# An attention and expert kernel on Trainium2: one weight piece per tile, the pieces' clamp on GpSimd, new charges in the planner, and the split of scores and value products four tiles earlier

## The chip, the cores and the metric

The kernel runs on one core of a Trainium2 chip. The metric is device time in microseconds of one execution. The engines are named as in the profile: PE is TensorE (its weight loads are PEld), DVE is VectorE, ACT is ScalarE, POOL is GpSimd, SP is SyncE, whose queue issues all DMAs here. The runs of the kernel before took 870.15 us in the median of three (869.43 to 871.0).

## What is computed

```python
k_all, v_all = concat(k_g, k_l), concat(v_g, v_l)          # 32 global and 512 local keys
out_g = softmax(q_g @ k_all.T / 8) @ v_all                 # 8 batches x 8 heads, head size 64
s_ll = where(abs(i - j) <= 32, q_l @ k_l.T / 8, -1e9)
out_l = softmax(concat(q_l @ k_g.T / 8, s_ll)) @ v_all
x = concat(out_g, out_l)  -> 8 x 544 tokens of 512
h = maximum(maximum(x @ w1, x @ w2), x @ w3)               # 512 -> 768
out = h @ w_out                                            # 768 -> 512
```

All activations are float32. The four expert weights come in as float64, 24 pieces of 128x512 in all (18 of w1 to w3, 6 of w_out), and are turned into pairs of rounded values on the chip.

## The kernel before

**Tiles.** Two heads make a pair, and a pair's 512 local queries make four tiles of 128. So there are 128 tiles, sixteen to a batch. For each tile the kernel computes scores of both heads against a window of at most 224 keys (`scores`), reduces them on DVE with the mask, the sign and the minimum (line 314), takes the exponential on ACT (316), scales on whatever engine the planner picks, mostly POOL (112), and sends the result by DMA into a padded tile `early` or `prob` (322). PE transposes that (334), the copy `pt` leaves PSUM (`trans`), the global queries' part is transposed and joined (`transg`, 355), and `pv` multiplies by the values (375 or 382). Once per pair `glob` and `glob_soft` do the global queries' scores, softmax and six DMAs into `probg`. At every fourth tile the pair's result is split for the experts (`split_x`, tile xs).

**Native and split products.** PE multiplies either plain float32 (`native`, lines 265, 307 and 375) or values split into a rounded high half and a rest (lines 269, 311 and 382). Splitting needs a copy and a subtraction for queries (qs), keys (kst), values (vs) and probabilities (pt), and for the value products three additions behind (388, 390). `NATK` holds the tiles whose scores are native, `NAT` the number of tiles whose value products are. Before, scores are native up to tile 27 and value products up to tile 25.

**Experts.** `moe_group` does a batch's three products and the maximum (413, 421), splits the result (h), and does the second product (432). It is a generator, of which `fill` runs 18 steps in each tile, one batch behind the attention: the first batch's experts start at tile 16. The weights of its block f are needed from about tile 16 + 2f, the second product's from tile 28.

**Weight pieces.** `convert` loads a piece (512 KB, tile wraw) and rebuilds float32 values from the float64 bits: the modulus on ACT (167), the clamp (168), the mask and shift (169) and two combinations (170, 171) on DVE. A step later it makes the high half (`copy`) and the rest (`sub`), wh and wl or woh and wol. `weight_step` finishes one piece, computes the next and loads another. `WS` says how many steps follow each tile. The load tiles share the buffers h0 to h5 with the experts: first six of them, later three, two and one.

**What sets the order.** The code issues work in the order of the tile loop, and a scheduler orders each engine's instructions from that. `copy`, `sub` and `times` choose their engine by charges kept in `load`: the engine with the least sum takes the work, and `spend` charges what is done without a choice. All engines work off their own queues in order. An instruction that waits holds up those behind it on its engine, and a DMA that waits on SP holds up the later ones.

Of the kernel before, what the change touches and what calls it, by code (L numbers as in the profile page):

```python
# [10 lines left out]
F32R = mybir.dt.float32r  # L11
# [3 lines left out]
ALU = mybir.AluOpType  # L15
# [4 lines left out]
DM, DF = 512, 768  # L20
# [2 lines left out]
KW = 576  # L23
NEG = -8.0e9

NATK = range(0, 28)
HIMAX = float(np.array(0x47EFFFFF, np.int32).view(np.float32))


# [18 lines left out]
def f32(ap):  # L48
    return ap.bitcast(F32)


def body(ctx, tc, kin, qin, vin, min_, w1, w2, w3, w4, out):
    nc = tc.nc
    act, dve, pool, pe = nc.scalar, nc.vector, nc.gpsimd, nc.tensor
# [21 lines left out]
    def spend(e, ns):  # L76
        load[e] += ns
# [18 lines left out]
    def copy(out, a, psum=False):  # L96
        n = width(out)
        c = {"d": n * (1.04 if psum else 0.52) + (160 if psum else 150), "a": n * 0.833 + (150 if psum else 190)}
        if least(c) == "d":
            dve.tensor_copy(out=out, in_=a)  # L100
        else:
            act.copy(out=out, in_=a)  # L102
# [32 lines left out]
    wo = []  # L135
# [3 lines left out]
    def pieces():  # L139
        n = 0  # L140
        for f in range(12):
            for i in range(3 if f < 6 else 1):
                if f < 6:
                    src = (w1, w2, w3)[i][:, f * 128:(f + 1) * 128].rearrange("(k p) f -> p k f", p=128)
                    yield src, 4, n, wh[f][:, i].rearrange("p k f -> p (k f)"), wl[f][:, i].rearrange("p k f -> p (k f)")
                else:
                    if f == 6:
                        wo.extend(const.tile([128, 6, DM], F32R, name=t, tag=t) for t in ("woh", "wol"))
                    yield w4[(f - 6) * 128:(f - 5) * 128], 1, n, wo[0][:, f - 6], wo[1][:, f - 6]
                n += 1  # L150

    def STAGE(n):
# [5 lines left out]
    def convert(piece):  # L158
        src, k, m, dh, dl = piece
        n, i = 512, STAGE(m)  # L160
        r = moe.tile([128, n], mybir.dt.int64, name="wraw", tag=f"h{i}")
        nc.sync.dma_start(out=r.rearrange("p (k f) -> p k f", k=k) if k > 1 else r, in_=src)
        hi = r.bitcast(I32).rearrange("p (n t) -> p n t", t=2)[:, :, 1]
        lo = r.bitcast(I32).rearrange("p (n t) -> p n t", t=2)[:, :, 0]
        yield
        c = cut[:, m % 6] if m < 18 else moe.tile([128, n], I32, name="wct", tag="o", bufs=2)
        act.activation(out=f32(c), in_=r.bitcast(F32).rearrange("p (n t) -> p n t", t=2)[:, :, 1], func=AF.Abs)
        dve.tensor_scalar(out=f32(c), in0=f32(c), scalar1=2.0 ** -15, scalar2=HIMAX, op0=ALU.max, op1=ALU.min)
        dve.tensor_scalar(out=c, in0=c, scalar1=0x07FFFFFF, scalar2=3, op0=ALU.bitwise_and, op1=ALU.logical_shift_left)
        dve.scalar_tensor_tensor(out=hi, in0=hi, scalar=-0x40000000, in1=c, op0=ALU.bitwise_and, op1=ALU.bitwise_or)  # L170
        dve.scalar_tensor_tensor(out=c, in0=lo, scalar=29, in1=hi, op0=ALU.logical_shift_right, op1=ALU.bitwise_or)
        spend("a", 520)
        spend("d", 1900)
        yield
        copy(dh, f32(c))
        sub(dl, f32(c), f32(dh))
        yield
# [20 lines left out]


    NS = 4 * B * NP  # L200
    NAT = 26
    EARLY, AHEAD = 16, 9
    kraw, kst, qraw, qs, vraw, vs, xr, sc, pg, pts = [{} for _ in range(10)]

# [49 lines left out]
    def glob(p, step):  # L254
        if p >= B * NP:
            return
        if step == 0:
            pg[p] = [att.tile([64, KW], F32, name="sg", bufs=1)[:, 0:NG], small.tile([64, 2], F32, name="nmg"), small.tile([64, 2], F32, name="zg")]
        s, nm, z = pg[p]
        c0, n = SEG[step]  # L260
        s0 = 384 * step
        ps = psS.tile([128, 512], F32, name="S")
        if 4 * p in NATK:

            pe.matmul(ps[0:64, 0:n], lhsT=kraw[p][:, KW:KW + 2 * SG], rhs=kraw[p][:, c0:c0 + n], start=True, stop=True)  # L265
            in1 = zero[0:64].to_broadcast([64, n])
        else:
            for j in range(2):
                pe.matmul(ps[:, 0:n], lhsT=qgz.rearrange("p j x -> p (j x)")[:, 128 * j:128 * j + 128],  # L269
                          rhs=kst[p][:, j, c0:c0 + n], start=(j == 0), stop=(j == 1))  # L270
            in1 = s[:, s0:s0 + n]
            copy(in1, ps[64:128, 0:n], True)
        dve.tensor_tensor_reduce(out=s[:, s0:s0 + n], in0=ps[0:64, 0:n], in1=in1, scale=-0.125, scalar=3.0e38,  # L273
                                 op0=ALU.add, op1=ALU.min, accum_out=nm[:, step:step + 1])
        spend("d", n * 1.04 + 75)

    def glob_soft(p):
        if p >= B * NP:
# [13 lines left out]
    def scores(sl):  # L292
        if sl >= NS:
            return
        p, t = divmod(sl, 4)
        c0, n = WIN[t]

        ps = pm.tile([128, 512], F32, name="pm") if sl < 12 else psS.tile([128, 512], F32, name="S")
        s = att.tile([128, 2, 224], F32, name="s", bufs=4)
        sc[sl] = early[:, sl % 6] if sl < EARLY else prob[sl % 2]  # L300
        nm = small.tile([128, 2], F32, name="nm")
        z = small.tile([128, 2], F32, name="z")
        ph = [ps[:, 0:224], ps[:, 224:448]]
        for j in range(2):
            if sl in NATK:

                pe.matmul(ph[j][:, 0:n], lhsT=qraw[sl][:, 128 * j:128 * j + 128], rhs=kraw[p][:, c0:c0 + n],  # L307
                          start=True, stop=True)
                continue
            for a in range(2):  # L310
                pe.matmul(ph[j][:, 0:n], lhsT=qs[sl][:, a, 128 * j:128 * j + 128],  # L311
                          rhs=kst[p][:, j, c0:c0 + n], start=(a == 0), stop=(a == 1))
        for j in range(2):
            dve.tensor_tensor_reduce(out=s[:, j, 0:n], in0=ph[j][:, 0:n], in1=mask[:, (1, 0, 1, 0)[t], 32 * (t == 0):32 * (t == 0) + n],  # L314
                                     scale=-0.125, scalar=3.0e38, op0=ALU.add, op1=ALU.min, accum_out=nm[:, j:j + 1])
            act.activation(out=s[:, j, 0:n], in_=s[:, j, 0:n], func=AF.Exp, bias=nm[:, j:j + 1], scale=-1.0,  # L316
                           accum_out=z[:, j:j + 1])
        dve.tensor_scalar(out=z, in0=z, scalar1=1e-9, scalar2=None, op0=ALU.add)
        dve.reciprocal(out=z, in_=z)
        for j in range(2):  # L320
            times(s[:, j, 0:n], s[:, j, 0:n], z[:, j:j + 1])
        nc.sync.dma_start(out=f32(sc[sl])[:, :, 0:n], in_=s[:, :, 0:n])
        spend("d", 2 * (n * 1.04 + 75) + 150)
        spend("a", 2 * (n * 0.833 + 278))

    def trans(sl):
# [130 lines left out]

    mm = [None]

    WS = [0, 0, 0, 1, 0, 1, 0, 1, 0, 1, 0, 1, 2, 2, 1, 2, 2, 1, 2, 2, 1, 2, 2, 1, 2, 2]  # L460

    def fill(n):
        if mm[0]:
# [34 lines left out]
    for sl in range(NS):  # L498
        p, t = divmod(sl, 4)
# [84 lines left out]
```

## Time and profile before

| what | value |
|---|---|
| runs | 870.15 us (869.43 to 871.0) |
| profiled execution, its own time | 868.76 us |
| its span, first to last instruction | 867.0 us |
| PE busy | 817.3 us (94%) |
| DVE, ACT, POOL busy | 617.3, 492.0, 502.9 us |
| mean granted clock of PE | 0.968 |

The span is that of the instructions; the execution's own time has 1.8 us around it. In the tables of busy time, a column is an engine's busy time in the stretch, and in brackets the number of its instructions; behind them stand the granted clock of PE as a share of full speed, the mean busy share of the 16 DMA engines, and GB/s. In the groups by shape, the row gives line, engine, operation, output and inputs, shape, count, then busy us and mean ns of one, then the idle time of the engine just before, with who ended it. A wait row gives the total, the number and the longest, in us.

### The profile page before, as it was taken

Reading aid. Unit: us, or ns where it says so; the run is one execution under the profiler, and the core shown is the slowest. Engines: PE = TensorE matmul, PEld = TensorE weight load, DVE = VectorE, ACT = ScalarE, POOL = GpSimd, SP = SyncE. Lnnn points to the kernel's source line nnn. Section 1 sums busy time; section 2 is a strip of 40 time slices with the busy share of each in tenths; the row PEclk is TensorE's granted clock in tenths of the full one; section 3 lists DMA queues with packets and bytes.
Section 4 is the critical chain, followed back from the end, with each engine's and each line's share of the span. In section 5 each row is a group of like instructions: output and inputs, shape, how many; then the busy total and the mean of one; then the engine's idle time right before and its main releaser. Section 6 shows DMA issues by size and latency. Waiting matters only on the chain.

```text
span 867.0 us, 15698 instructions
## 1 busy us (share of the span) xinstructions
PE 817.3 (94%) x4452; PEld 677.3 (78%) x4452; DVE 617.3 (71%) x1885; ACT 492.0 (57%) x1392; POOL 502.9 (58%) x669
## 2 busy tenths in 40 slices
PE   5865988799999999999999999999999999999997
PEld 3643766588888788888887888888888888888897
DVE  4678897887788787887788887877877877521111
ACT  3654655566666566766666666666666666411111
POOL 4544657576667666776767666756677665411211
PEclk8876889899999999999999999999999999999999
DMA  6676755334333533343333433353333422100000
GB/s 202 192 222 197 212 182 158 117 93 144 99 101 104 160 110 105 99 133 114 103 107 104 142 102 98 101 161 104 111 110 122 122 78 74 62 24 1 25 25 25
DMA packets 107238, 98.53 MB, mean 114 GB/s; under 512 B 21008, under 2 KB 97936, under 8 KB 107152
## 3 DMA queue, kind: packets, MB, share of 16 engines
q1 hardware_dynamic: 107152, 97.53, 37.0%
q8 instruction: 36, 0.59, 0.3%
q14 instruction: 50, 0.41, 0.2%
HBM read 56.85 MB, written 8.91 MB: 76 GB/s over the span
## 4 chain that ended last, share of the span: by engine, by line
PE 77%; DVE 10%; DMA 6%; issue 2%; POOL 2%; ACT 1%; SPq 1%; DVEq 0%; POOLq 0%; ACTq 0%
PE pm L413 45%; PE pm L432 13%; PE O L382 6%; PE S L311 5%; PE T L334 3%; DMA wraw<-w_in 1%; DMA wraw<-wo_in 1%; PE S L269 1%; DVE wraw L170 1%; DVE xs L100 1%; PE S L265 1%; PE S L355 1%; PE O L375 1%; DVE s L314 1%; DVE kst L94 1%
## 5 line engine op out<-in xcount | busy, mean ns | idle before, releaser
L413 PE MATMUL pm<-xs,wh 128*128 128x512 f32 (+1 forms) x1296 | 411.2, 390 | 0.0
L413 PEld LDWEIGHTS pm<-xs,wh 128*128 128x128 f32 x1296 | 235.3, 191 | 31.6
L413 PE MATMUL pm<-xs,wl 128*128 128x512 f32 (+1 forms) x648 | 254.9, 393 | 0.0
L112 POOL TENSOR_SCALAR s<-s,z 128x224 f32<-128x224 f32 (+1 forms) x243 | 111.6, 472 | 87.7 <-ACT lox L102 46.7
L316 ACT ACTIVATE s<-s,nm 128x192 f32<-128x192 f32 (+1 forms) x256 | 118.0, 462 | 48.6 <-DVE nm L314 44.0
L413 PEld LDWEIGHTS pm<-xs,wl 128*128 128x128 f32 x648 | 123.6, 191 | 23.5 <-issue 2.4
L432 PE MATMUL pm<-woh,h 128*128 128x512 f32 x408 | 135.2, 400 | 1.3 <-POOL h L94 1.1
L94 POOL TENSOR_TENSOR h<-m,h 128x512 fp32r<-128x512 f32 (+1 forms) x54 | 69.3, 1284 | 99.2 <-ACT h L102 99.2
L94 POOL TENSOR_TENSOR qs<-qraw,qs 128x256 fp32r<-128x256 f32 x100 | 79.5, 795 | 68.6 <-ACT qs L102 42.0
L421 DVE TENSOR_TENSOR m<-pm,m 128x512 f32<-128x512 f32 (+1 forms) x108 | 71.0, 657 | 63.0 <-PE pm L413 62.7
L94 DVE TENSOR_TENSOR pt<-T,pt 128x512 fp32r<-128x512 f32 x102 | 70.4, 691 | 36.2 <-ACT pt L102 33.8
L432 PEld LDWEIGHTS pm<-woh,h 128*128 128x128 f32 x408 | 74.6, 188 | 15.4 <-POOL h L94 4.3
L314 DVE CUSTOM_DVE_ANT_0 s<-S,mask 128x192 f32<-128x192 f32 (+1 forms) x232 | 77.5, 370 | 9.9 <-PE S L307 5.2
L432 PE MATMUL pm<-wol,h 128*128 128x512 f32 x204 | 81.7, 401 | 0.0
L94 POOL TENSOR_TENSOR vs<-vraw,vs 128x256 fp32r<-128x256 f32 x102 | 75.7, 743 | 9.0 <-ACT vs L102 4.2
L102 ACT CAST pt<-T 128x512 fp32r<-128x512 f32 x83 | 48.4, 583 | 47.6 <-PE T L334 47.6
L382 PEld LDWEIGHTS O<-pt,vs 128*128 128x128 f32 x408 | 66.4, 188 | 9.2
L382 PE MATMUL O<-pt,vs 128*128 128x320 f32 (+1 forms) x408 | 72.8, 299 | 0.0
L102 ACT CAST qs<-qraw 128x256 fp32r<-128x256 f32 x85 | 34.6, 407 | 64.3 <-PE S L311 64.0
L334 PEld LDWEIGHTS T<-identr,prob 128*128 128x128 f32 x448 | 51.3, 143 | 24.9 <-issue 5.0
L311 PEld LDWEIGHTS S<-kst,qs 128*128 128x128 f32 x400 | 59.5, 190 | 11.2 <-DVE nmg L273 2.8
L102 ACT CAST h<-m 128x512 fp32r<-128x512 f32 (+1 forms) x54 | 32.3, 597 | 60.5 <-DVE m L421 60.4
(99 smaller groups left out, 1340.5 us busy)
## 6 DMA issues: line engine op xcount, KB each, us to landing
vraw<-v_in SPq DMA_DIRECT2D x128, 128.0 KB, 2.6
qraw<-q_in SPq DMA_DIRECT2D x100, 128.0 KB, 2.2
prob<-s SPq DMA_DIRECT2D x56, 224.0 KB, 2.4
prob<-s SPq DMA_DIRECT2D x56, 192.0 KB, 2.3
wraw<-w_in SPq DMA_DIRECT2D x18, 512.0 KB, 4.5
out_dram<-o SPq DMA_DIRECT2D x32, 256.0 KB, 2.6
kraw<-k_in SPq DMA_DIRECT2D x25, 320.0 KB, 3.1
qn<-q_in SPq DMA_DIRECT2D x28, 128.0 KB, 3.5
```

Source lines behind the costliest of these rows:

```text
L94: (dve if least(c) == "d" else pool).tensor_tensor(out=out, in0=a, in1=b, op=ALU.subtract)
L100: dve.tensor_copy(out=out, in_=a)
L102: act.copy(out=out, in_=a)
L112: pool.tensor_scalar(out=out, in0=a, scalar1=col, scalar2=1.0, op0=ALU.mult, op1=ALU.mult)
L311: pe.matmul(ph[j][:, 0:n], lhsT=qs[sl][:, a, 128 * j:128 * j + 128], rhs=kst[p][:, j, c0:c0 + n], start=(a == 0), stop=(a == 1))
L314: dve.tensor_tensor_reduce(out=s[:, j, 0:n], in0=ph[j][:, 0:n], in1=mask[:, (1, 0, 1, 0)[t], 32 * (t == 0):32 * (t == 0) + n], scale=-0.12 ...
L316: act.activation(out=s[:, j, 0:n], in_=s[:, j, 0:n], func=AF.Exp, bias=nm[:, j:j + 1], scale=-1.0, accum_out=z[:, j:j + 1])
L334: i = pe.transpose(pr[:, 256 * j + 128 * c:256 * j + 128 * c + 128], s[:, j, 128 * c:128 * c + 128], identr)
L382: pe.matmul(o[:, j, 0:320].rearrange("p (a q) -> p a q", a=2)[:, :, 0:n], lhsT=vs[sl][:, 2 * j + c].rearrange("p a d -> p (a d)"), rhs=pt[ ...
L413: pe.matmul(ps[:, 0:n], lhsT=w[f][:, i, k], rhs=xs[k][:, a, 0:n], start=(q == 0), stop=(q == 11))
L421: dve.tensor_tensor(out=m[:, 0:n], in0=ps[:, 0:n], in1=m[:, 0:n], op=ALU.max)
L432: pe.matmul(ps, lhsT=hh[f][:, a, 128 * t:128 * t + 128], rhs=w[:, f], start=(q == 0), stop=(q == 17))
```

## The change

Five edits stand together.

1. `WS` gives one weight step behind each of the tiles 1 to 25, where it gave none up to tile 2, one behind every second tile up to 11, and then two, two and one in turn. Before, 24 pieces are through at tile 23, now at tile 25.
2. The clamp of a piece (before line 168) is issued on POOL, not on DVE. The instruction is the same, a maximum with one constant and a minimum with another.
3. The planner's charges change: a piece is charged 650 to ACT, 900 to POOL and 2100 to DVE (520 and 1900 before, nothing to POOL); a score reduction is charged 220 beyond its columns where it was 75, and the small reciprocal work 440 where it was 150. Since DVE's sum rises faster, `copy`, `sub` and `times` pick ACT and POOL more often, in the whole kernel.
4. `NAT` falls from 26 to 22 and `NATK` from 28 to 24 tiles: four tiles more have split value products and four more have split scores.
5. The tiles woh and wol are made when the first piece of w_out is finished, not when it is loaded.

```diff
--- before.py
+++ after.py
@@ -23,7 +23,7 @@
 KW = 576
 NEG = -8.0e9
 
-NATK = range(0, 28)
+NATK = range(0, 24)
 HIMAX = float(np.array(0x47EFFFFF, np.int32).view(np.float32))
 
 
@@ -144,9 +144,7 @@
                     src = (w1, w2, w3)[i][:, f * 128:(f + 1) * 128].rearrange("(k p) f -> p k f", p=128)
                     yield src, 4, n, wh[f][:, i].rearrange("p k f -> p (k f)"), wl[f][:, i].rearrange("p k f -> p (k f)")
                 else:
-                    if f == 6:
-                        wo.extend(const.tile([128, 6, DM], F32R, name=t, tag=t) for t in ("woh", "wol"))
-                    yield w4[(f - 6) * 128:(f - 5) * 128], 1, n, wo[0][:, f - 6], wo[1][:, f - 6]
+                    yield w4[(f - 6) * 128:(f - 5) * 128], 1, n, f - 6, None
                 n += 1
 
     def STAGE(n):
@@ -165,13 +163,18 @@
         yield
         c = cut[:, m % 6] if m < 18 else moe.tile([128, n], I32, name="wct", tag="o", bufs=2)
         act.activation(out=f32(c), in_=r.bitcast(F32).rearrange("p (n t) -> p n t", t=2)[:, :, 1], func=AF.Abs)
-        dve.tensor_scalar(out=f32(c), in0=f32(c), scalar1=2.0 ** -15, scalar2=HIMAX, op0=ALU.max, op1=ALU.min)
+        pool.tensor_scalar(out=f32(c), in0=f32(c), scalar1=2.0 ** -15, scalar2=HIMAX, op0=ALU.max, op1=ALU.min)
         dve.tensor_scalar(out=c, in0=c, scalar1=0x07FFFFFF, scalar2=3, op0=ALU.bitwise_and, op1=ALU.logical_shift_left)
         dve.scalar_tensor_tensor(out=hi, in0=hi, scalar=-0x40000000, in1=c, op0=ALU.bitwise_and, op1=ALU.bitwise_or)
         dve.scalar_tensor_tensor(out=c, in0=lo, scalar=29, in1=hi, op0=ALU.logical_shift_right, op1=ALU.bitwise_or)
-        spend("a", 520)
-        spend("d", 1900)
+        spend("a", 650)
+        spend("p", 900)
+        spend("d", 2100)
         yield
+        if m >= 18:
+            if not wo:
+                wo.extend(const.tile([128, 6, DM], F32R, name=t, tag=t) for t in ("woh", "wol"))
+            dh, dl = [w[:, dh] for w in wo]
         copy(dh, f32(c))
         sub(dl, f32(c), f32(dh))
         yield
@@ -198,7 +201,7 @@
 
 
     NS = 4 * B * NP
-    NAT = 26
+    NAT = 22
     EARLY, AHEAD = 16, 9
     kraw, kst, qraw, qs, vraw, vs, xr, sc, pg, pts = [{} for _ in range(10)]
 
@@ -272,7 +275,7 @@
             copy(in1, ps[64:128, 0:n], True)
         dve.tensor_tensor_reduce(out=s[:, s0:s0 + n], in0=ps[0:64, 0:n], in1=in1, scale=-0.125, scalar=3.0e38,
                                  op0=ALU.add, op1=ALU.min, accum_out=nm[:, step:step + 1])
-        spend("d", n * 1.04 + 75)
+        spend("d", n * 1.04 + 220)
 
     def glob_soft(p):
         if p >= B * NP:
@@ -320,7 +323,7 @@
         for j in range(2):
             times(s[:, j, 0:n], s[:, j, 0:n], z[:, j:j + 1])
         nc.sync.dma_start(out=f32(sc[sl])[:, :, 0:n], in_=s[:, :, 0:n])
-        spend("d", 2 * (n * 1.04 + 75) + 150)
+        spend("d", 2 * (n * 1.04 + 220) + 440)
         spend("a", 2 * (n * 0.833 + 278))
 
     def trans(sl):
@@ -457,7 +460,7 @@
 
     mm = [None]
 
-    WS = [0, 0, 0, 1, 0, 1, 0, 1, 0, 1, 0, 1, 2, 2, 1, 2, 2, 1, 2, 2, 1, 2, 2, 1, 2, 2]
+    WS = [0] + [1] * 25
 
     def fill(n):
         if mm[0]:
```

Line numbers behind line 147 move by up to 3: the clamp is line 166, mask and combinations are 167 to 169, the score reduction 317.

DVE's order just behind the sum over the columns of tile 7 (xg, line 392). `cut` and `wraw` are a piece in work, `wh` its high half, `s<-S,mask` a score reduction. Before:

```order
L392 TENSOR_REDUCE xg<-xr 128x32
L100 CAST wh_102<-cut 128x512
L168 TENSOR_SCALAR cut<-cut 128x512
L169 TENSOR_SCALAR cut<-cut 128x512
L170 SCALAR_TENSOR_TENSOR wraw<-wraw,cut 128x512
L171 SCALAR_TENSOR_TENSOR cut<-wraw 128x512
L100 CAST wh_103<-cut 128x512
L100 COPY pt<-S 128x2x32
L314 ISA s,nm<-S,mask 128x224
```

Now:

```order
L395 TENSOR_REDUCE xg<-xr 128x32
L167 TENSOR_SCALAR cut<-cut 128x512
L168 SCALAR_TENSOR_TENSOR wraw<-wraw,cut 128x512
L169 SCALAR_TENSOR_TENSOR cut<-wraw 128x512
L167 TENSOR_SCALAR cut<-cut 128x512
L168 SCALAR_TENSOR_TENSOR wraw<-wraw,cut 128x512
L169 SCALAR_TENSOR_TENSOR cut<-wraw 128x512
L317 ISA s,nm<-S,mask 128x224
```

Two pieces stand where one stood, without their clamps, and the casts and the copy of pt have gone from DVE.

POOL's order around the tiles 16 to 20, from the softmax of the global queries of the pair (sg) on. `wl`, `wol` are pieces' low halves, `kst`, `qs`, `qgz` are halves of keys and queries, `h` is of the experts. Before:

```order
L112 TENSOR_SCALAR sg<-sg,zg 64x544
L112 TENSOR_SCALAR s<-s,z 128x224 x2
L94 TENSOR_TENSOR wl_112<-cut,wh_106 128x512
L94 TENSOR_TENSOR qgz<-kraw,qgz 128x2x32
L94 TENSOR_TENSOR wl_113<-cut,wh_107 128x512 x2
L112 TENSOR_SCALAR s<-s,z 128x224 x2
L94 TENSOR_TENSOR h_1159<-m,h_1159 128x512
L94 TENSOR_TENSOR kst<-kraw,kst 64x576 x2
L94 TENSOR_TENSOR wl_113<-cut,wh_107 128x512
L112 TENSOR_SCALAR s<-s,z 128x192 x2
```

Now, from the first keys of the pair whose scores are split:

```order
L94 TENSOR_TENSOR kst<-kraw,kst 64x576 x2
L94 TENSOR_TENSOR wl_113<-cut,wh_107 128x512
L112 TENSOR_SCALAR s<-s,z 128x192 x2
L166 TENSOR_SCALAR cut<-cut 128x512 x2
L112 TENSOR_SCALAR sg<-sg,zg 64x544
L94 TENSOR_TENSOR h_1033<-m,h_1033 128x512
L94 TENSOR_TENSOR wl_113<-cut,wh_107 128x512
L94 TENSOR_TENSOR qs<-qraw,qs 128x256
L166 TENSOR_SCALAR wct<-wct 128x512
L112 TENSOR_SCALAR s<-s,z 128x224 x2
```

The clamps stand among the scalings and the low halves, one or two at a time, and the keys and queries of the split tiles come before the last pieces of w1 to w3 are finished.

## The prediction, on record before the result

> **What bounds the kernel now.** I read the page first (DVE, ACT and POOL are all partly idle, PE is not), then the table of busy time by stage, then the waits of PE in the stage in which the change lies, then the groups of instructions by shape. The stages are cut where the work changes. Up to 92.1 us stand the attention tiles 0 to 15, from there to 172.7 us the tiles 16 to 25, which run beside the first batch's expert layer, and behind 172.7 us everything is split attention beside expert matmuls, with a tail of experts alone.
>
> ```profile
> core 0: us, PE busy (x) PEld busy (x) DVE busy (x) ACT busy (x) POOL busy (x), PEclk, DMA share, GB/s
> 0.00:92.10 92.10, 60.23 (x326) 43.32 (x326) 62.88 (x221) 48.17 (x148) 45.12 (x67) 0.78 0.67 199
> 92.10:172.70 80.60, 70.32 (x363) 53.00 (x363) 68.30 (x162) 45.15 (x122) 52.22 (x53) 0.92 0.55 170
> 172.70:750.00 577.30, 574.49 (x3163) 483.73 (x3162) 464.43 (x1462) 379.62 (x1086) 388.51 (x533) 1.00 0.37 111
> 750.00:867.00 117.00, 112.27 (x605) 97.25 (x603) 21.66 (x43) 19.07 (x39) 17.07 (x18) 1.00 0.07 22
> ```
>
> I call these stages A (92.1 us), B (80.6 us), C and the tail. That A holds sixteen tiles and B ten is read from the native value products of line 375, eight records a tile (one straddles the cut):
>
> ```profile
> 0.00:92.10 92.10, 16.37 (x129) 10.36 (x129) 0.78 0.67 199
> 92.10:172.70 80.60, 7.37 (x80) 4.69 (x80) 0.92 0.55 170
> ```
>
> In C, PE is busy 574.49 of 577.30 us at full clock: there nothing but PE's own work counts. In A and B PE idles and its granted clock sinks to 0.78 and 0.92. So the change can pay only ahead of 172.7 us, or in what it takes off PE. What a tile costs when PE alone sets the pace is read where it is busy without a break, with the counts of line 375 and of the split value products of line 382 (four a tile) for the same stretches:
>
> ```profile
> 92.10:111.60 19.50, 19.50 (x110) 15.10 (x109) 16.88 (x44) 12.58 (x34) 11.82 (x12) 1.00 0.82 248
> 301.90:394.90 93.00, 92.76 (x513) 78.39 (x512) 74.72 (x238) 61.64 (x179) 64.30 (x88) 1.00 0.38 114
> ...
> 92.10:111.60 19.50, 2.18 (x24) 1.40 (x24) 1.00 0.82 248
> 301.90:394.90 93.00, 11.41 (x64) 10.41 (x64) 1.00 0.38 114
> ```
>
> Three native tiles take 19.50 us, 6.50 each. Sixteen split ones take 93.0, 5.81 each. Ten native tiles at 6.50 are 65.0 us, so B loses 15.6 of its 80.6 us to waits and to the low clock behind them. Who is waited for there, longest first:
>
> ```profile
> PE S L355 <- DVE nm L314: 3.0, 2, 2.1
> PE S L355 <- DMA probg<-sg: 2.8, 1, 2.8
> ```
>
> DVE is named, and it is busy 68.30 of 80.60 us in B, 0.85, the highest share of any engine but PE. What fills it is the conversion of weight pieces, by its clamps (line 168) in A, in B, and in two stretches of four tiles in A:
>
> ```profile
> 0.00:92.10 92.10, 6.84 (x11) 0.78 0.67 199
> 92.10:172.70 80.60, 10.87 (x13) 0.92 0.55 170
> 44.30:62.20 17.90, 1.08 (x2) 0.71 0.74 218
> 62.20:82.20 20.00, 2.54 (x4) 0.73 0.73 230
> ```
>
> **The change part by part.** Durations, from the groups by shape:
>
> ```profile
> L94 POOL TENSOR_TENSOR qs<-qraw,qs 128x256 fp32r<-128x256 f32 x100 | 79.5, 795 | 68.6 <-ACT qs L102 42.0 <-DMA qraw<-q_in 8.6 <-DVE nm L314 5.1
> L94 POOL TENSOR_TENSOR vs<-vraw,vs 128x256 fp32r<-128x256 f32 x102 | 75.7, 743 | 9.0 <-ACT vs L102 4.2 <-DVE z L318 1.7 <-DVE vs L100 1.7
> ...
> L94 POOL TENSOR_TENSOR wl<-cut,wh 128x512 fp32r<-128x512 f32 x18 | 24.3, 1352 | 19.8 <-ACT wh L102 13.6 <-DVE wh L100 5.7 <-DVE z L318 0.4
> ...
> L112 POOL TENSOR_SCALAR sg<-sg,zg 64x544 f32<-64x544 f32 x32 | 23.0, 719 | 40.5 <-ACT pt L102 26.6 <-ACT o L102 7.3 <-DVE zg L284 4.3
> ...
> L170 DVE SCALAR_TENSOR_TENSOR wraw<-wraw,cut 128x512 int32<-128x512 int32 x18 | 16.5, 917 | 0.3
> ...
> L168 DVE TENSOR_SCALAR cut<-cut 128x512 f32<-128x512 f32 x18 | 12.9, 718 | 3.5 <-ACT cut L167 3.4
> ...
> L167 ACT ACTIVATE cut<-wraw 128x512 f32<-128x512 f32 x18 | 12.1, 674 | 7.7 <-DMA wraw<-w_in 7.7
> ...
> L169 DVE TENSOR_SCALAR cut<-cut 128x512 int32<-128x512 int32 x18 | 10.9, 605 | 0.2
> ...
> L102 ACT CAST wh<-cut 128x512 fp32r<-128x512 f32 x12 | 7.4, 618 | 14.6 <-DVE cut L171 14.5
> ```
>
> *The clamp.* No clamp of 128x512 runs on POOL before. Its ends are the same kind of instruction on 544 columns, 0.72 us, and POOL's two-input instruction on 512, 1.35. I take 0.69, the first one scaled to 512 columns and rounded up, since kind and inputs are the same. So POOL gains 24 x 0.69 = 16.6 us and DVE loses the clamps, 6.84 + 10.87 = 17.7. DVE's mask (old line 169) now waits for POOL, and behind it in DVE's order stand the score reductions, for which the exponentials, the probability DMAs and PE's transposes wait.
>
> *The pieces' tiles.* By DVE's order 15 pieces are masked before the sum that ends tile 15; the trace has 11 clamps in A. So A carries 4 more pieces, B 4 fewer, and each also moves its 512 KB load on SP's queue ahead of the probability DMAs. What a piece more costs A: four tiles with two pieces took 17.90 us, four with four took 20.00, so 1.05 us a piece, 4.2 for four. The ends: 0 if all of it hides in engines that are at most 0.68 busy in A, and, if POOL became the pace, its added work, 4 x 1.35 + 15 x 0.69 = 15.8. I take 4.2, the row nearest to it.
>
> *B.* Six native tiles at 6.50 and four split ones at 5.81 are 62.2 us of PE work, against 65.0. How much of the 15.6 us of loss stays? DVE's load falls: 68.3, less 10.9 of clamps, less 4 pieces x (0.605 + 2 x 0.917, with line 171 taken as line 170) = 9.8, is 47.6. The split tiles' sums on DVE and the casts that the new charges take from DVE stand against each other; I set them equal. POOL's rises: 52.2 + 9 x 0.69 for clamps, less 6 low halves of pieces x 1.35 (8 of them in its order behind tile 15's split, against 14 in B before), plus four query and four value low halves, 4 x 1.54, plus one pair's keys, 2 x 1.5 by columns (576 to 512, from wl): 59.5. DVE gets slack and POOL becomes the next to be late, with 59.5 of 62.2. It can push some query and value halves past 172.7 us, where it is 388.51 of 577.30 busy. I take half the loss as left, 8 us (ends 0 and 15.6): B is 70.2, a gain of 10.4.
>
> *C and the tail.* Copies move to ACT, over sixty by the order, 0.2 to 0.7 us each. ACT is 379.62 of 577.30 busy there, DVE 464.43: the load is levelled and PE's work is the same. 0, give or take 1. That cover is gone only if a late copy on ACT holds PE's one transposition buffer.
>
> *The sum.* The profiled execution took 868.76 us, its span 867.0. 868.76 + 4.2 - 10.4 = 862.6. It stands 1.4 below the median of the runs, 870.15, so in the runs' terms 864.0. About 0.2% (1.7 us) is what a measurement of this kernel can tell from no change.
>
> **The rivals.** *First, slower: DVE and POOL take turns.* On DVE the clamp took 3.00 us at 111.01, while POOL ran instructions back to back, and the mask behind it 0.43:
>
> ```profile
> 111.01 3.00 DVE L168 TENSOR_SCALAR cut<-cut 128x512 f32<-128x512 f32 x1
> 114.04 0.43 DVE L169 TENSOR_SCALAR cut<-cut 128x512 int32<-128x512 int32 x1
> ...
> 111.58 0.88 POOL L112 TENSOR_SCALAR s<-s,z 128x224 f32<-128x224 f32 x2
> 112.44 1.28 POOL L94 TENSOR_TENSOR wl<-cut,wh 128x512 fp32r<-128x512 f32 x1
> ```
>
> If the two exclude each other, the clamp still occupies both, now 0.69 instead of 0.43, and each mask starts just when POOL has taken its next instruction, up to 1.35 us long. If so, A pays its 4.2 and some 0.4 us for each of 15 pieces, 6.0, and in B POOL's 59.5 us and DVE's waits leave the loss whole, so only 65.0 - 62.2 = 2.8 is won: 870.15 + 4.2 + 6.0 - 2.8 = 877.6. It decides against the change from 6.2 / 24 = 0.26 us a piece on the path. Against it: DVE's slack, 47.6 of 62.2 in B, can take such waits. The Trainium skill (SBUF — State Buffer, section Who interferes with whom) says that DVE's fast-mode or two-SBUF-input instructions and GpSimd's share a port pair as an exclusive lock, so that the second "fully blocks". By that rule alone a piece holds the pair 0.26 us longer, 24 x 0.26 = 6.2, and the sum would be 870.2. The rows above agree that DVE waits; whether it is on the path no row of before can show.
>
> *Second, no change: A gives back what B wins.* By its order ACT takes the casts of the pieces and the copies in A that DVE had, about 18 instructions of at most 0.62, plus 4 x 0.674 of moduli and 4 more casts: at most 16.4 us on 48.17. If 10 us of it end on the path, A is 10 longer and the sum is 870. For it: the exponentials stand in the same queue. Against it: 65 of 92.1 us.
>
> *Third, faster than forecast: the load hides.* A costs nothing, and only 3 of B's 15.6 us stay: 80.6 - 65.2 = 15.4, so 854.8. For it: DVE is the engine waited for, and it is relieved in both stages.
>
> **How the numbers follow.** The forecast (858 to 868) 0.46, the load hides 0.19, no change 0.12, the turns 0.23. Faster by over 0.2% is forecast and third, 0.65; same 0.12; slower 0.23. The range leaves out what lies beyond the third case's centre by little, 0.06, and the upper half of the first rival, 0.12: 854 to 875.
>
> **What would show it.** Right: the first split value products start near 166.5 us instead of 172.7 (six earlier), tile 16's native ones near 96, DVE's share in B falls below 0.80, and the waits of PE for DVE's reductions shrink; C keeps 577 us for the same matmuls. The 0.69 is read from the new group of clamps on POOL. Wrong: masks with a mean well above 0.605 us or idle DVE ahead of them with POOL as releaser (first rival), transposes waiting for ACT in A (second), or a C in which PE idles.

## The result and the profile after

The changed kernel took 900.51 us in the median of four runs (899.76 to 901.21), the kernel before 869.88 in the runs beside it: a ratio of 1.035 [1.0332, 1.0368], 30.6 us slower. The forecast was 864.0, and the range ended at 875.

The profiled execution after took 899.76 us with a span of 898.0, and a mean granted clock of 0.949 (0.968 before). Its table of busy time, cut at the same points of the work (tile 16, tile 26, the end of the attention):

```profile
core 0: us, PE busy (x) PEld busy (x) DVE busy (x) ACT busy (x) POOL busy (x), PEclk, DMA share, GB/s
0.00:117.80 117.80, 64.45 (x328) 44.18 (x328) 60.81 (x203) 58.98 (x175) 77.29 (x84) 0.71 0.56 172
117.80:205.60 87.80, 71.00 (x345) 53.96 (x346) 55.46 (x146) 49.04 (x134) 66.83 (x65) 0.88 0.42 130
205.60:781.00 575.40, 573.46 (x3164) 484.09 (x3164) 428.84 (x1386) 407.42 (x1154) 395.97 (x547) 1.00 0.37 112
781.00:898.00 117.00, 112.27 (x605) 97.10 (x603) 21.94 (x43) 19.07 (x39) 17.07 (x18) 0.99 0.06 22
```

Stage A is 117.8 us against 92.1 (+25.7), B 87.8 against 80.6 (+7.2), C 575.4 against 577.3 (-1.9), and the tail is the same. All the loss lies ahead of tile 26. POOL, the least busy of the engines in A before, is now the fullest there: 77.29 of 117.80 us, against 45.12 of 92.10. DVE does less in A and B than before and stands more. What it stands for is in the groups by shape:

```profile
L166 POOL TENSOR_SCALAR cut<-cut 128x512 f32<-128x512 f32 x18 | 35.0, 1949 | 6.5 <-ACT cut L165 5.6
...
L167 DVE TENSOR_SCALAR cut<-cut 128x512 int32<-128x512 int32 x18 | 13.7, 762 | 38.1 <-POOL cut L166 38.1
...
L166 POOL TENSOR_SCALAR wct<-wct 128x512 f32<-128x512 f32 x6 | 11.5, 1920 | 5.2 <-ACT wct L165 4.0 <-DMA probg<-sg 1.1
...
L167 DVE TENSOR_SCALAR wct<-wct 128x512 int32<-128x512 int32 x6 | 4.6, 775 | 17.8 <-POOL wct L166 17.8
```

A clamp on POOL takes 1.92 to 1.95 us, not 0.69. The 24 of them fill 46.5 us of POOL, and the masks (now line 167) wait 38.1 + 17.8 = 55.9 us for them. The waits between 23 and 206 us, longest first, carry it on:

```profile
DVE cut L167 <- POOL cut L166: 34.7, 13, 4.9
ACT wh L102 <- DVE cut L169: 28.1, 11, 5.8
...
PE O L378 <- ACT pt L102: 19.6, 4, 10.7
DVE wct L167 <- POOL wct L166: 17.8, 6, 4.3
```

DVE waits for POOL, ACT's cast of the high half waits for DVE, and PE waits for a copy of pt that stands behind that cast on ACT. Before, the value products had waited for such copies, up to 206 us:

```profile
PE O L375 <- ACT pt L102: 0.9, 1, 0.9
PE O L375 <- DVE pt L100: 0.8, 1, 0.8
```

The longest of the waits after the change are seen in the timeline around 60 us (start, duration, engine and line, in brackets the idle time ahead and its releaser):

```profile
58.61 3.80 POOL L166 TENSOR_SCALAR cut<-cut 128x512 f32<-128x512 f32 x2
63.63 1.50 POOL L94 TENSOR_TENSOR wl<-cut,wh 128x512 fp32r<-128x512 f32 x1 [1.22 <-ACT wh L102]
...
60.56 0.83 DVE L167 TENSOR_SCALAR cut<-cut 128x512 int32<-128x512 int32 x1 [4.91 <-POOL cut L166]
...
64.05 1.63 DVE L169 SCALAR_TENSOR_TENSOR cut<-wraw 128x512 int32<-128x512 int32 x1
65.61 0.38 DVE L317 CUSTOM_DVE_ANT_0 s<-S,mask 128x224 f32<-128x224 f32 x1
...
62.93 0.62 ACT L102 CAST wh<-cut 128x512 fp32r<-128x512 f32 x1 [5.79 <-DVE cut L169]
65.72 0.62 ACT L102 CAST wh<-cut 128x512 fp32r<-128x512 f32 x1 [2.17 <-DVE cut L169]
66.24 0.20 ACT L102 COPY pt<-S 128x64 f32<-128x64 f32 x1
...
66.50 0.80 PE L378 MATMUL O<-pt,vraw 128*64 128x160 f32 x4 [10.75 <-ACT pt L102]
```

Two clamps stand one behind the other on POOL. DVE is idle for 4.91 us until the first is done, so nothing of DVE's can have stretched that first one. The two pieces then hold DVE until 65.6 and ACT until 66.2, and the short copy that PE has been waiting for since 55.75 comes behind them. Before, that copy was on DVE and tile 7 took 8.5 us to the next tile's value products; now it takes 17.1.

### The profile page after: what moved, and what is told of

The parts are those of the page before. It is cut to its first block, busy times and chain, and to the rows that moved or that the text cites. A ratio compares the mean times of both kernels' runs of the same rounds, so it can differ in the third digit from the quotient of the medians.

```text
span 898.0 us, 15754 instructions
## 1 busy us (share of the span) xinstructions
PE 821.2 (91%) x4436; PEld 679.3 (76%) x4436; DVE 567.0 (63%) x1777; ACT 534.5 (60%) x1500; POOL 557.2 (62%) x713
## 4 chain that ended last, share of the span: by engine, by line
PE 76%; POOL 3%; DVE 2%; DMA 2%; ACT 1%; issue 1%; SPq 0%; POOLq 0%; DVEq 0%; ACTq 0%
PE pm L416 45%; PE pm L435 14%; PE O L385 6%; PE S L314 5%; PE T L337 3%; PE S L272 1%; DMA prob<-s 1%; POOL wct L166 1%; ACT s L319 1%; PE S L358 1%; DVE wraw L168 1%; DVE z L321 0%; DVE wct L167 0%; POOL wol L94 0%; POOL h L94 0%
## 5 line engine op out<-in xcount | busy, mean ns | idle before, releaser
L112 POOL TENSOR_SCALAR s<-s,z 128x224 f32<-128x224 f32 (+1 forms) x245 | 108.6, 456 | 79.0 <-ACT lox L102 38.0
L94 DVE TENSOR_TENSOR pt<-T,pt 128x512 fp32r<-128x512 f32 x106 | 73.1, 690 | 52.1 <-ACT pt L102 50.5
L321 DVE TENSOR_SCALAR z<-z 128x2 f32<-128x2 f32 x128 | 55.6, 434 | 58.7 <-ACT s L319 58.4
L102 ACT CAST pt<-T 128x512 fp32r<-128x512 f32 x100 | 58.5, 585 | 48.4 <-PE T L337 47.6
L94 POOL TENSOR_TENSOR vs<-vraw,vs 128x256 fp32r<-128x256 f32 x106 | 78.8, 743 | 12.0 <-ACT vs L102 10.0
L385 PEld LDWEIGHTS O<-pt,vs 128*128 128x128 f32 x424 | 69.0, 188 | 13.3 <-POOL s L112 2.3
L385 PE MATMUL O<-pt,vs 128*128 128x320 f32 (+1 forms) x424 | 76.0, 300 | 3.1 <-DVE xr L393 1.9
L94 POOL TENSOR_TENSOR kst<-kraw,kst 64x576 fp32r<-64x576 f32 x52 | 75.7, 1455 | 4.1
L102 ACT CAST qs<-qraw 128x256 fp32r<-128x256 f32 x104 | 42.3, 407 | 53.0 <-PE S L314 51.6
```

The source lines that it names most:

```text
L94: (dve if least(c) == "d" else pool).tensor_tensor(out=out, in0=a, in1=b, op=ALU.subtract)
L112: pool.tensor_scalar(out=out, in0=a, scalar1=col, scalar2=1.0, op0=ALU.mult, op1=ALU.mult)
L385: pe.matmul(o[:, j, 0:320].rearrange("p (a q) -> p a q", a=2)[:, :, 0:n], lhsT=vs[sl][:, 2 * j + c].rearrange("p a d -> p (a d)"), rhs=pt[ ...
```

## The experiments

All times are medians. "Tile 16" and "tile 26" are the starts of these tiles' value products in the profiled execution, "rest" is its span behind the start of tile 26. That is one execution for each kernel; those of e2 and e12 lie 2.8 and 3.5 us above their medians.

| kernel | us (lowest to highest) | ratio to before, 95% | tile 16 | tile 26 | rest |
|---|---|---|---|---|---|
| before | 870.15 (869.43 to 871.0) | | 92.1 | 172.7 | 694.3 |
| after | 900.51 (899.76 to 901.21) | 1.035 [1.0332, 1.0368] | 117.8 | 205.6 | 692.4 |
| e1, clamp back on DVE | 874.68 (873.61 to 875.15) | 1.0054 [1.0035, 1.0073] | 104.7 | 180.8 | 692.1 |
| e2, clamp alone | 896.3 (895.94 to 899.1) | 1.0309 [1.0281, 1.0337] | 107.4 | 199.6 | 697.3 |
| e3, pieces alone | 870.25 (869.87 to 872.29) | 1.0009 [0.9995, 1.0024] | 101.3 | 175.1 | 694.1 |
| e4, multiplication on POOL | 877.3 (876.67 to 878.62) | 1.0086 [1.0061, 1.011] | 106.4 | 182.8 | 692.1 |
| e5, splits alone | 874.41 (873.23 to 876.37) | 1.0057 [1.0043, 1.0071] | 89.0 | 178.0 | 693.4 |
| e6, charges alone | 863.31 (862.72 to 865.76) | 0.9928 [0.9915, 0.9942] | 92.5 | 170.2 | 690.7 |
| e7, three forms | 890.19 (one run) | | 111.8 | 196.2 | 692.2 |
| e8, masks a step later | 903.31 (902.7 to 904.27) | 1.0383 [1.037, 1.0397] | 117.1 | 207.8 | 693.1 |
| e9, clamps of nothing | 888.15 (887.14 to 888.41) | 1.0205 [1.0179, 1.023] | 108.9 | 193.0 | 692.4 |
| e10, charges and pieces | 869.9 (866.05 to 872.2) | 0.999 [0.9975, 1.0006] | 105.6 | 177.0 | 691.8 |
| e11, charges and splits | 870.74 (867.12 to 873.09) | 1.0002 [0.9988, 1.0017] | 91.6 | 176.7 | 691.4 |
| e12, charges, splits later | 863.19 (861.2 to 866.7) | 0.992 [0.9898, 0.9943] | 93.6 | 170.5 | 694.4 |
| e13, e10 with casts on DVE | 868.67 (867.03 to 871.67) | 0.9988 [0.9977, 0.9999] | 100.1 | 174.7 | 691.9 |
| e14, after with casts on DVE | 903.62 (901.97 to 904.27) | 1.0387 [1.037, 1.0403] | 118.1 | 210.0 | 692.0 |
| e15, e6 with casts on DVE | 865.04 (864.13 to 867.93) | 0.9955 [0.9937, 0.9972] | 93.6 | 171.8 | 690.7 |

### The clamp: undone, and alone (e1, e2)

```diff
 e1, against after:
-        pool.tensor_scalar(out=f32(c), in0=f32(c), scalar1=2.0 ** -15, scalar2=HIMAX, op0=ALU.max, op1=ALU.min)
+        dve.tensor_scalar(out=f32(c), in0=f32(c), scalar1=2.0 ** -15, scalar2=HIMAX, op0=ALU.max, op1=ALU.min)
 e2, against before:
-        dve.tensor_scalar(out=f32(c), in0=f32(c), scalar1=2.0 ** -15, scalar2=HIMAX, op0=ALU.max, op1=ALU.min)
+        pool.tensor_scalar(out=f32(c), in0=f32(c), scalar1=2.0 ** -15, scalar2=HIMAX, op0=ALU.max, op1=ALU.min)
```

> The changed kernel with the clamp back on DVE, all else as changed. Theory (length): the clamp takes 1.94 us on POOL against 0.72 on DVE, DVE waits 52.5 us for it in front of the masks, and what stands behind the masks in DVE's and ACT's orders carries that to PE. Then nearly all of the 30 us come back: 860 to 872 us. First rival (pieces): four more pieces in the first sixteen tiles and the copies that the new charges send to ACT are what costs; then it stays at 885 us or above.

> The kernel before with the one edit that the clamp runs on POOL. Length: the whole loss shows here too, 24 clamps by 1.2 us longer, most of it on the path: 890 to 905 us. Pieces: the clamp is hidden in POOL's idle time, 868 to 874 us.

With the clamp back on DVE 25.8 of the 30.6 us are gone (900.51 to 874.68). The clamp alone, with nothing else changed, costs 896.3 - 869.9 = 26.4. The place of the clamp is the cause of most of the loss, whichever pieces, charges and splits stand around it. In e1 a clamp takes 0.5 to 0.6 us on DVE:

```profile
L166 DVE TENSOR_SCALAR cut<-cut 128x512 f32<-128x512 f32 x18 | 10.6, 590 | 2.6 <-ACT cut L165 2.6
...
L166 DVE TENSOR_SCALAR wct<-wct 128x512 f32<-128x512 f32 x6 | 3.1, 512 | 8.5 <-ACT wct L165 8.5
```

### What of the clamp costs: its length or its place (e4, e7)

```diff
 e4, against after:
-        pool.tensor_scalar(out=f32(c), in0=f32(c), scalar1=2.0 ** -15, scalar2=HIMAX, op0=ALU.max, op1=ALU.min)
+        pool.tensor_scalar(out=f32(c), in0=f32(c), scalar1=1.0, scalar2=1.0, op0=ALU.mult, op1=ALU.mult)
 e7, against after:
-        pool.tensor_scalar(out=f32(c), in0=f32(c), scalar1=2.0 ** -15, scalar2=HIMAX, op0=ALU.max, op1=ALU.min)
+        if m % 3 == 0:
+            pool.tensor_scalar(out=f32(c), in0=f32(c), scalar1=2.0 ** -15, scalar2=1.0, op0=ALU.max, op1=ALU.mult)
+        elif m % 3 == 1:
+            pool.tensor_scalar(out=f32(c), in0=f32(c), scalar1=HIMAX, scalar2=1.0, op0=ALU.min, op1=ALU.mult)
+        else:
+            pool.tensor_scalar(out=f32(c), in0=f32(c), scalar1=1.0, scalar2=0.0, op0=ALU.mult, op1=ALU.add)
```

> The changed kernel with the clamp's two operations, maximum and minimum, replaced by two multiplications with 1.0 on POOL; the clamping of the pieces is left out. It stands in the same place with the same operands in size. Length by kind of operation: the instruction falls from 1.94 to about 0.7 us as the softmax scaling of 544 columns does, and the time to 862 to 875 us. Second rival (place): the way over POOL's queue costs whatever the instruction's length; then 888 us or above, with DVE's masks still waiting tens of us for POOL. If the instruction stays at 1.9 us, its length does not come from the kind of operation, and the time stays at 900.

> The changed kernel with the clamp on POOL taken apart: every third piece has the maximum and a multiplication with 1.0, the next the minimum and a multiplication, the third a multiplication and an addition of 0; so each piece lacks one or both bounds of the clamp. Length by kind of operation: a maximum and a minimum cost POOL about 0.65 us more each than a multiplication, so 1.2 to 1.3 us for the first two and 0.63 for the third. If one of the two alone is slow, its group shows 1.9 and the other 0.6.

In e4 the same kind of instruction on the same 128x512 values, but with two multiplications, takes 0.62 to 0.63 us on POOL:

```profile
L167 DVE TENSOR_SCALAR cut<-cut 128x512 int32<-128x512 int32 x18 | 12.8, 712 | 19.4 <-POOL cut L166 19.4
...
L166 POOL TENSOR_SCALAR cut<-cut 128x512 f32<-128x512 f32 x18 | 11.3, 630 | 8.3 <-ACT cut L165 8.3
...
L167 DVE TENSOR_SCALAR wct<-wct 128x512 int32<-128x512 int32 x6 | 4.6, 772 | 10.0 <-POOL wct L166 10.0
```

The time falls to 877.3, so 900.5 - 877.3 = 23.2 us come from the length of the operation. What is left of the move, the hop over POOL and back with 19.4 + 10.0 = 29.4 us of masks waiting, costs 877.3 - 874.7 = 2.6. So the total of a wait is no price: 29.4 us of it cost 2.6 here, and 55.9 cost 25.8 in the changed kernel. In e7 the three forms stand beside each other in one execution:

```profile
L169 POOL TENSOR_SCALAR cut<-cut 128x512 f32<-128x512 f32 x6 | 11.7, 1943 | 1.6 <-ACT cut L165 1.2
L167 POOL TENSOR_SCALAR cut<-cut 128x512 f32<-128x512 f32 x6 | 11.5, 1920 | 1.2 <-ACT cut L165 1.2
...
L171 POOL TENSOR_SCALAR cut<-cut 128x512 f32<-128x512 f32 x6 | 4.0, 659 | 3.5 <-ACT cut L165 3.4
```

One minimum with a multiplication (line 169) takes 1.94 us, one maximum with a multiplication (167) 1.92, a multiplication with an addition (171) 0.66. The expectation that one of the two would cost half was wrong: a single maximum or minimum already costs the whole.

### How a long clamp reaches PE (e8, e9, e14)

```diff
 e8, against after (the masks a step behind the clamp, one step more in WS):
         pool.tensor_scalar(out=f32(c), in0=f32(c), scalar1=2.0 ** -15, scalar2=HIMAX, op0=ALU.max, op1=ALU.min)
+        yield
...
+        if masked:
+            next(masked.pop())
...
-            next(live.pop())
+            masked.append(live.pop())
+            next(masked[0])
...
-    WS = [0] + [1] * 25
+    WS = [0] + [1] * 26
 e9, against after (clamp on DVE; a dummy on a tile of its own, behind POOL's last low half or scaling):
...
-        pool.tensor_scalar(out=f32(c), in0=f32(c), scalar1=2.0 ** -15, scalar2=HIMAX, op0=ALU.max, op1=ALU.min)
+        dve.tensor_scalar(out=f32(c), in0=f32(c), scalar1=2.0 ** -15, scalar2=HIMAX, op0=ALU.max, op1=ALU.min)
+        with tc.issue_after(last[0].ins):
+            last[0] = pool.tensor_scalar(out=idle, in0=idle, scalar1=2.0 ** -15, scalar2=HIMAX, op0=ALU.max, op1=ALU.min)
 e14, against after:
-        copy(dh, f32(c))
+        least({"d": 512 * 0.52 + 150, "a": 512 * 0.833 + 190})
+        dve.tensor_copy(out=dh, in_=f32(c))
```

> The changed kernel with the clamp still on POOL at 1.9 us, but the masks and all behind them on DVE one weight step later, so that the clamp has a tile's time to end; one step more, behind tile 26, finishes the last piece. If the loss is DVE standing at the masks: DVE's idle time ahead of the masks falls from 52.5 us to under 15, and the time to 872 to 882 us. If POOL's 46 us of clamps are themselves what is late (scalings and low halves behind them): 888 us or above, with the masks no longer waiting.

> The clamp back on DVE, as in the run that gave 874.7 us, and beside it 24 clamps of the same size and kind on POOL, on a tile that nobody else reads or writes, each standing behind a low half or a scaling in POOL's order. So POOL has the changed kernel's load and DVE waits for none of it. If the loss is DVE standing at the masks: 874 to 884 us. If POOL's occupation is what costs (scalings and low halves late, and DVE kept off while POOL works): 890 us or above.

> The changed kernel, clamp on POOL, with the cast of a piece's high half always on DVE and the charges left as they were. Theory (DVE's standing at the masks reaches PE by way of the casts that wait on ACT ahead of copies of pt and exponentials): PE's 19.6 us of waits for copies of pt on ACT fall below 8, and the time falls by 8 to 13, to 888 to 893, near the 888.2 of the clamps that nobody waits for. Rival (it reaches PE by DVE's own queue, the score reductions behind the masks): masks still wait some 50 us, PE waits for the reductions or for the probability DMAs in place of ACT, and the time stays within 3 us of 900.5.

e8 doesn't answer its question. The scheduler put the masks just behind their clamps again, and they still waited 43.0 + 14.8 us, where under 15 had been expected. So its 903.31 tells nothing of what a mask that doesn't wait would give.

e9 keeps POOL at least as busy as the change does, with 24 clamps for which nobody waits, and costs 888.15 - 874.68 = 13.5 us over e1. The remaining 900.51 - 888.15 = 12.4 are what it costs more when the chain of a piece runs through the clamp. DVE's standing at the masks is the part of that which the trace shows; that it is all of it is a difference of two runs and not shown by itself, since in the changed kernel POOL too waits 6.5 + 5.2 us ahead of its clamps, and the dummies only 1.5. Neither theory had this half and half. The dummies are the longest group on POOL up to tile 26, and PE's waits there name what came late:

```profile
L175 POOL TENSOR_SCALAR idle<-idle 128x512 f32<-128x512 f32 x24 | 48.9, 2037 | 1.5
```

```profile
PE T L346 <- DMA prob<-s: 14.6, 6, 5.4
PE S L367 <- DMA probg<-sg: 10.5, 3, 3.8
PE O L387 <- ACT pt L109: 10.4, 5, 5.6
```

The same waits in e1:

```profile
PE O L378 <- ACT pt L102: 7.3, 3, 4.3
PE T L337 <- DMA prob<-s: 7.2, 3, 4.0
...
PE S L358 <- DMA probg<-sg: 3.3, 1, 3.3
```

PE waits 14.6 us for `prob`, against 7.2 in e1, and 10.5 for `probg`, against 3.3. The probability DMAs wait for scalings (POOL's line 119 in e9, 112 in e1) that queue behind the dummies. On SP's queue, from 23 us to tile 26, e9 first and then e1:

```profile
SPq L334 <- POOL s L119: 45.5, 17, 9.5
```

```profile
SPq L325 <- POOL s L112: 31.4, 15, 6.2
```

DVE's own instructions on a piece aren't stretched in one direction (clamp 590 to 698 ns, mask 838 to 715), and all of them together take 75.4 us against 72.9; DVE's whole busy time up to tile 26 is 132.5 against 130.4. So nothing shows that a DVE held up by POOL is more than a small part of the 13.5.

The theory that the half with the masks comes to PE through ACT's casts alone fell with e14. With every cast on DVE, the value products' waits for copies on ACT fall from 19.6 us to 2.4, but others take their place, and the time is 903.62, 3.1 us more than the changed kernel and just beyond the 3 that the rival allowed:

```profile
PE S L359 <- DVE nm L318: 24.8, 6, 9.2
PE T L338 <- DMA prob<-s: 12.1, 3, 6.5
```

The masks still wait 38.2 + 12.5 us, and the score reductions behind them in DVE's queue are what PE waits for. So two queues behind the mask are late, and when ACT's is freed, DVE's is next. The other way round wasn't run.

### The other three edits (e3, e5, e6, e10, e11)

```diff
 e3 and e10, against before:
-    WS = [0, 0, 0, 1, 0, 1, 0, 1, 0, 1, 0, 1, 2, 2, 1, 2, 2, 1, 2, 2, 1, 2, 2, 1, 2, 2]
+    WS = [0] + [1] * 25
 e5 and e11, against before:
-NATK = range(0, 28)
+NATK = range(0, 24)
...
-    NAT = 26
+    NAT = 22
 e6, e10 and e11, against before:
-        spend("a", 520)
-        spend("d", 1900)
+        spend("a", 650)
+        spend("p", 900)
+        spend("d", 2100)
...
-        spend("d", n * 1.04 + 75)
+        spend("d", n * 1.04 + 220)
...
-        spend("d", 2 * (n * 1.04 + 75) + 150)
+        spend("d", 2 * (n * 1.04 + 220) + 440)
```

> The kernel before with the one edit that a weight step follows each of the tiles 1 to 25. Length: this alone does little, 865 to 875 us. Pieces: 880 us or above, with most of it ahead of the sixteenth tile.

> The kernel before with the one edit that value products are split from tile 22 on and scores from tile 24 on. PE does four tiles at 5.81 instead of 6.50 us, 2.8 less; DVE, ACT and POOL do four tiles' splitting more, while the last weight pieces are converted. If PE sets the pace there: 867 us. If the other engines do (what is left of the loss when the clamp is back on DVE, 4.7 us, then lies here): 873 to 876 us.

> The kernel before with the one edit of the planner's charges: DVE is charged more, and copies go to ACT and POOL. If levelling the engines is harmless or good, as the forecast had it: 867 to 871 us. If copies of the probabilities that now stand in ACT's queue behind casts of weight pieces are late for PE (the changed kernel's trace has PE wait 19.6 us for them ahead of the value products): 873 to 880 us, with that wait back in the trace.

> The charges, which gave 863.3 us alone, with one weight piece a tile, which gave 870.3 alone (no difference). If the two add up: 863 to 865 us. If the 4.7 us that stay with the clamp on DVE come from these two together (ACT takes more copies and more pieces early): 868 to 873 us.

> The charges, 863.3 us alone, with the splits four tiles earlier, 874.4 alone. If the two add up: 867 to 869 us. If the relieved DVE makes the splits free, PE's 2.8 us are won: 860 to 863 us.

Alone, the pieces change nothing that is clear of noise (+0.3 us), the splits cost 4.5, and the charges win 6.6. The busy times of e3 up to tile 26:

```profile
0.00:101.30 101.30, 62.22 (x326) 43.90 (x327) 70.55 (x231) 53.56 (x159) 53.64 (x69) 0.73 0.63 196
101.30:175.10 73.80, 66.37 (x361) 50.50 (x362) 58.31 (x149) 39.16 (x110) 46.55 (x53) 0.98 0.54 166
```

A pays 9.2 us for the earlier pieces and B gives 6.8 of it back, at a granted clock of 0.98. For the splits, the tiles 16 to 21 and 22 to 25 of e5, and the same tiles before:

```profile
89.00:141.30 52.30, 41.67 (x219) 31.62 (x219) 47.32 (x101) 31.06 (x81) 42.93 (x39) 0.93 0.60 187
141.30:178.00 36.70, 27.10 (x129) 21.54 (x128) 31.12 (x78) 21.76 (x60) 23.05 (x28) 0.91 0.35 109
```

```profile
92.10:138.00 45.90, 42.53 (x221) 32.23 (x220) 41.99 (x94) 26.84 (x71) 29.18 (x29) 0.93 0.65 202
138.00:172.70 34.70, 27.79 (x145) 20.77 (x145) 26.32 (x69) 18.31 (x52) 23.05 (x25) 0.90 0.42 128
```

PE's busy time falls by 1.55 us (70.32 to 68.77). DVE's in B rises by 10.1 (68.31 to 78.44) and POOL's by 13.8 (52.23 to 65.98), and PE's idle time in B doubles, from 10.28 to 20.23. The splits take a little off PE and put far more on DVE and POOL, and PE waits for what these deliver. For the charges, e6:

```profile
0.00:92.50 92.50, 61.58 (x325) 44.06 (x325) 57.52 (x208) 54.04 (x165) 44.52 (x65) 0.74 0.65 199
92.50:170.20 77.70, 68.70 (x363) 51.69 (x363) 62.30 (x147) 48.22 (x131) 49.63 (x48) 0.95 0.55 172
170.20:860.90 690.70, 684.92 (x3766) 581.25 (x3764) 447.10 (x1431) 425.16 (x1191) 411.99 (x564) 1.00 0.32 97
```

DVE has 566.9 us of work in all instead of 617.3, and the time comes back in B (80.6 to 77.7) and behind it (694.3 to 690.7), where the prediction had set 0.

The edits do not add. On top of the charges the pieces cost 6.6 us (863.31 to 869.90) and the splits 7.4 (to 870.74). In the order charges, pieces, splits, clamp the way from before to after is -6.6 (e6), +6.6 (e10), +4.8 (e1, which has edit 5 too), +25.8 (after). Edit 5 was not run by itself.

### Why pieces and charges collide (e13, e15)

The edit is that of e14, made to e10 and to e6.

> Charges and one weight step a tile, and the cast that makes a piece's high half is always issued on DVE, behind the combination that it reads, while the planner is still charged as it was, so that all other choices stay. Theory (ACT's queue: a cast that waits for DVE holds the copies of pt behind it): PE's waits ahead of tile 16 for copies of pt on ACT fall from 11.6 us to below 4, tile 16 starts some 5 us earlier than the 105.6 of the run without this, and the time is 863 to 866. Rival (ahead of tile 16 the added pieces themselves are the load, on whatever engine): the waits move to DVE's reductions and the time stays at 868 to 872.

> The control: the new charges alone, with the cast of a piece's high half always on DVE. PE waits there only 2.2 us for copies of pt on ACT ahead of tile 16, so by the theory of ACT's queue there is nothing to win: within 1.5 us of the 863.3 of the charges alone, or up to 2 us slower, since DVE is 0.80 busy in the tiles 16 to 25 and takes 16 casts of at most 0.49 us more. If it is over 2 us faster, the cast's place pays on its own and e13 says nothing on the one step a tile.

PE's waits ahead of tile 16 for copies of pt on ACT were 4.8 us with the pieces alone, 8.5 + 3.1 with both:

```profile
PE O L376 <- ACT pt L102: 8.5, 3, 5.6
...
PE T L335 <- ACT pt L102: 3.1, 4, 1.4
```

With the casts on DVE neither of them is among PE's seven longest waits up to 206 us, the shortest of which is 2.6, and tile 16 starts at 100.1 instead of 105.6, as the theory of ACT's queue had it. But the time, 868.67, lies in the rival's range. It is only 1.2 us below e10's 869.90, and the two spread over nearly the same times. Against the control, which the casts on DVE cost 1.7 us (863.31 to 865.04), the pieces now cost 868.67 - 865.04 = 3.6 instead of 6.6. By that ACT's queue would be about 3 of the 6.6; but the 3 are a difference of differences between kernels whose runs spread over 3 to 6 us, so they are not shown. That the waits on ACT go and tile 16 starts earlier is shown, and for the rest no cause was found.

### A version that beats both (e12)

```diff
 e12, against e6:
-NATK = range(0, 28)
+NATK = range(0, 32)
...
-    NAT = 26
+    NAT = 30
```

> The charges with the splits four tiles later than before: value products native up to tile 29, scores up to tile 31. If the splitting work beside the last pieces is what costs, this wins again, 859 to 862 us. If PE sets the pace in those tiles by now, four tiles at 6.50 instead of 5.81 us cost 2.8: 866 us.

Moving the splits the other way wins nothing beyond the charges, 863.19 against 863.31, and neither expectation came true. Both beat the kernel before by 0.7 to 0.8% and the changed one by 4%. The simplest version with this time is the kernel before with the new charges alone.

## Why the prediction was wrong

**The step that failed first is the clamp's price.** "I take 0.69, the first one scaled to 512 columns" rested on rows of the same kind of instruction, on the same engine and near the same shape, but with another operation. It even had a ceiling, 1.35, from POOL's two-input instruction, and the truth lay at 1.92 to 1.95, above it. e4 shows that 0.69 was near enough for a multiplication (0.63). The row that could have warned was missing, since no maximum or minimum ran on POOL before, and the honest bound for an operation never seen there reached further up. The Trainium skill (GPSIMD Engine Reference, section 4.1 Engine selection) calls one-input work on GpSimd "roughly line-rate" and names maximum among such operations. The multiplication at 0.63 us bears that out beside the 0.51 to 0.59 of e1's clamp on DVE, the maximum and the minimum at 1.92 don't. Of the 36.5 us between 864.0 and 900.5, 23.2 are this length (e4).

**The price alone would not have saved it.** With an instruction of about the length that was taken, e4 still needs 877.3 us, 13.3 above the forecast and outside the range. So two more terms failed, A's +4.2 and B's -10.4. As spans, the forecast was 96.3 us for A, 70.2 for B and 694.3 for the rest. The changed kernel is 21.5 and 17.6 above it in A and B and 1.9 below in the rest; e4 is 10.1 and 6.2 above and 2.2 below.

**A, +4.2.** Two stretches of A that had differed in pieces gave 1.05 us a piece. The pieces alone cost A 9.2 (e3), 2.3 each, and all edits but the clamp 12.6 (e1). The second rival had named the place, ACT in A, and 10 us. Its sign came true (in the changed kernel's A, PE's transposes wait 5.8 us for ACT's copies of pt, 1.1 before), and e10 and e13 show such waits come and go with the casts on ACT; how much of the end time goes with them is not shown.

**B, -10.4.** Half of B's loss was to come back because clamps and pieces leave DVE. e3, which moves pieces and no clamp, loses 8.8 of its 73.8 us (ten native tiles at 6.50 are 65.0), where 8 were taken. So the size is met without the clamps, which is partly luck, and A pays all of it back in e3. PE's waits for DVE's reductions, from which DVE was read as what is late, had been 3.0 of PE's 10.28 idle us in B. The splits' share, 65.0 - 62.2 = 2.8 to the good, had the wrong sign (+4.5 alone, e5). It counted PE's own time and set the new work on DVE "equal" to the casts that leave it. With the clamp on POOL, B became 87.8, with PE's waits for DVE's reductions up to tile 26 at 10.0 us in place of 3.0.

**C, 0 give or take 1.** It came to -1.9, a little beyond its bounds, with PE busy 573.46 of 575.40. The charges were worth more than was set, 3.6 us behind tile 26 in e6.

**The signs that were named.** Tile 16 started at 117.8, not near 96, and the first split value products at 177.0, not 166.5. DVE's share in B fell below 0.80, to 55.46 of 87.80, but since DVE stood waiting: a low share of the engine that had been late was no proof that it was relieved. Masks with POOL as the releaser of idle DVE, the sign of the first rival, came true in 55.9 us. Its other sign, masks well above 0.605 us, came true too (0.76 and 0.78), but tells nothing: they take 0.84 in e1, where no clamp runs on POOL.

**The first rival.** It had the place and the side right, and the point from which it decides (0.26 us a piece; the masks waited 55.9 / 24 = 2.3). Its mechanism is not what was measured: the first of the two clamps at 58.61, half of their 3.80 us, ran beside an idle DVE, so its length doesn't come from taking turns. The rule of the Trainium skill that was weighed there (SBUF — State Buffer, section Who interferes with whom) gave 870.2; no run shows its lock as the cause of this loss, and none rules out a small part (in e9, DVE's work on the pieces is 2.5 us longer than in e1). That e4's 877.3 meets the rival's 877.6 is chance, since A and B of e4 are 106.4 and 76.4, not the rival's 102.3 and 77.8.

**What stays open.** How much of the 13.5 us of e9 is lateness of POOL's scalings and how much DVE's or ACT's own shift in order; why the pieces cost 3.6 us on top of the charges even with the casts on DVE; what edit 5 does by itself; and, with e8's failure, what the long clamp would cost if its masks stood far enough behind it.

## What to carry to other kernels

Carry a duration from one row to another only within the same operation, not just the same kind, engine and shape: here that made 0.69 us of 1.92. Time an operation that never ran on an engine by itself before moving 24 of them. An engine with slack in busy time still has a queue in order: an instruction that waits in it for a slower engine holds up all the later ones, and where two queues stand behind one wait (here DVE's reductions and ACT's copies), freeing one can show the other, as in e14. Edits of a planner's charges should be timed by themselves, since here they were the only part that paid, and the parts around them ate it.

## What the runs showed of the hardware

On POOL a one-input instruction on 128x512 float32 values takes 0.62 to 0.66 us in the mean with two multiplications or a multiplication and an addition (e4, e7), and 1.92 to 1.95 with a maximum or a minimum among its two operations (e7, after), three times as long. The dummies of e9 have a mean of 2.04, but the shortest take 1.91, as in the changed kernel. On DVE the same clamp has a mean of 0.51 to 0.59 us in e1 and of 0.72 to 0.80 before; half of them take 0.43 or less in e1. That one of the two operations is enough, and that the two don't add up, wasn't expected.
